# A scan and a bilinear feed-forward on one core: half of pair 1's B on GpSimd's load queue, third weights and middle rows behind its first mask

## The chip, the core and the metric

The kernel runs on one core of a Trainium2 chip. The metric is the device time of one execution in microseconds (us). The core has five engines with queues of their own: TensorE (PE, with its weight loads shown as PEld), VectorE (DVE), ScalarE (ACT), GpSimd (POOL) and SyncE (SP). Each works through its instructions in the order in which the program lists them and waits on semaphores for what other engines and transfers deliver. Transfers from memory (DMA) are issued by SP, ACT and GpSimd, and all three share the core's 16 DMA engines. In the profile a name with q behind it (SPq, ACTq) is the engine's sequencer.

## The reference

There are two parts, the second on the output of the first. With batch 4, 8 heads, 768 positions, head size 32 and state size 16:

```
log_a = log(clip(a, 1e-6, 1))
per chunk of 32 positions:
    cum  = cumsum(log_a of the chunk)
    L    = exp(cum_i - cum_j), lower triangle
    y    = ((C B^T) * L) x + (C state) * exp(cum)
    state = exp(sum log_a) * state + sum_j exp(cum_last - cum_j) B_j x_j
z   = y as 3072 tokens of 256 (head, dim)
out = ((z w_a) * (z w_b)) w_out        w_a, w_b: 256 x 1536, w_out: 1536 x 256
```

Inputs and the output are float32. The kernel computes products in float16 with float32 sums.

## The kernel before, in words

The 768 positions are cut in six blocks of 128 (`NBLK`); a block of two batches is a *pair*, so pairs 0 and 1 are block 0, pairs 2 and 3 are block 1, and so on up to pair 11. Decays come from a running product of `a` along a block (`scan`, line 250, on DVE) divided by its value in the middle (`over_mid`, line 253). For a pair, B and C are scaled by these factors (`scale_bc`, line 333, tiles `bm` and `cm`), turned on TensorE (`transposes`, line 374), multiplied to scores (`scores`, line 404) and masked (`mask`, lines 446 to 449). A mask is done by DVE straight from PSUM, or by GpSimd, and then ACT first copies the scores to `tmp`. The masked scores times x (`pv_u`, line 458) give `py`, and `evac0` (lines 563 and 565) copies it as float16 to `X2T`, on ACT or on DVE. From there the feed-forward takes units of 256 of the 1536 columns: `unit_mm` (line 598) makes `aps` with Wa and `bps` with Wb, `evac_a` (line 612) copies the one, `times` (line 622) multiplies both, and `out_mm` (line 637) multiplies with Wo.

The order of the work is written out by hand: the schedule is manual, and an engine does what is listed in the order of the listing. Four things in it matter here.

The loads come first. SP loads `a` and halves of pair 0's and pair 1's B (`bn`) and C (`cn`); ACT loads the other halves, five transfers, and then its activation table. GpSimd loads x of pair 0 in two halves (`xn`, 64 KB each), the first halves of Wa and Wb (384 KB each in float16), x of pair 1 in two halves, and the second half of Wa. Behind its first mask it loads the second half of Wb. In the calls `load1(engine, pair, which, half)`, which is 0 for B, 1 for C and 2 for x, and two further numbers limit a load to some rows.

Block 1 has layouts of its own: `load_q` loads its B and C (`bq`, `cq`) on SP. The first of these transfers is made to wait for the first half of Wa by a dependence on `w0`. `scale_q` (line 346, GpSimd) scales them into `planes`, `turn` (line 359, DVE) transposes them, and `scores(2)` uses them. `mid_rows` (line 288, GpSimd, tile `Ps`) makes the factors of block 1 and later, which `turned_rows` transposes. `clear` (line 294, GpSimd) sets the unused columns of the planes to zero.

Warmups (line 238) are matmuls of constants that nothing reads; they fill TensorE's queue at fixed places.

PSUM banks of the feed-forward are dealt out by the string `BANKS`: the n-th call of `bank` takes the n-th digit's bank, and a new user of a bank waits for the readers of the one before. The first calls are fps, tb, tc, py0, py1, and then aps of the first three units.

Of the kernel before, what the change touches and what calls it, by code (L numbers as in the profile page):

```python
# [19 lines left out]
SS = 64.0  # L20

BANKS = (
    "012313213212312312031203123021032103120312013201320130231021302130231203120312013023102310"
    "2312013201320132012301230123012301230123012301320132013201320132013201320132013201320"
)


# [1 line left out]
def kernel(  # L29
# [13 lines left out]
    nc = tc.nc  # L43
# [34 lines left out]
    Wa = [big.tile([128, 2, KC], f16, name=f"Wa{t}") for t in range(2)]  # L78
# [50 lines left out]
    def bank(name):  # L129
        return psf.tile([128, 512], f32, name=name, tag=f"ff{next(banks)}")  # L130
# [9 lines left out]
    def by_token(t_):  # L140
        return t_.rearrange("p h r n -> p (h r n)").rearrange("p (t h n) -> p t h n", t=2, h=H)

    def load1(eng, p, which, bt, i0=0, n=64, to=None):
        blk, bp = divmod(p, NBP)
        if p >= P2:
            return eng.dma_start(
                by_token(pair_in[p][which])[:, bt],
                (B, C, x)[which][2 * bp + bt, :, blk * Q : (blk + 1) * Q, :].rearrange("h q n -> q h n"),
            )
        src = (B, C, x)[which][2 * bp + bt, :, blk * Q + 2 * i0 : blk * Q + 2 * i0 + 2 * n, :]  # L150
        if to is None:
            to = pair_in[p][which]
        return eng.dma_start(
            to[64 * bt + i0 : 64 * bt + i0 + n].rearrange("i h r n -> i h (r n)"),
            src.rearrange("h (i r) n -> i h (r n)", r=2),
        )
# [3 lines left out]
    def load_q(eng, blk, parts=ALL_Q):  # L160
        if blk not in by_batch:
            by_batch[blk] = [inq.tile([128, H, 4, N], f32, name=n_, tag=n_) for n_ in ("bq", "cq")]
        return [
            eng.dma_start(
                by_batch[blk][w][32 * b : 32 * b + 32].rearrange("i h s n -> i h (s n)"),
                (B, C)[w][b, :, blk * Q : (blk + 1) * Q, :].rearrange("h (i s) n -> i h (s n)", s=4),
            )
            for w, b in parts
        ]
# [12 lines left out]
    def load_w(half, W):  # L182
        src = moe_w_a if W is Wa else moe_w_b
        c = slice(half * KC, (half + 1) * KC)
        return nc.gpsimd.dma_start(W[half], src.rearrange("(f p) e -> p f e", p=128)[:, :, c])
# [12 lines left out]
    load1(nc.scalar, 0, 1, 1)  # L198
    load1(nc.sync, 0, 1, 0, 0, 32)
    load1(nc.scalar, 0, 1, 0, 32, 32)  # L200
    for w in (1, 0):
        load1(nc.sync, 1, w, 0)
        load1(nc.scalar, 1, w, 1)
    nc.scalar.preload_act_table_set("natural_log_exp_and_others")
    nc.vector.memset(zero, 0.0)
    nc.gpsimd.memset(ident, 1.0)
# [21 lines left out]
    for p in range(2):  # L228
        for bt in range(2):
            load1(nc.gpsimd, p, 2, bt)  # L230
        if p == 0:
            w0 = load_w(0, Wa)
            load_w(0, Wb)
    load_w(1, Wa)

    def warmup(bank, *widths):
        for cols in widths:
# [10 lines left out]
    def scan(lo, hi):  # L248
        for k in range(lo, hi):
            nc.vector.tensor_tensor_scan(Pr[:, k], a_sb[:, k], zero, 1.0, ALU.mult, ALU.add)  # L250
# [4 lines left out]
    def sel_over_mid(lo, hi, eng):  # L255
        eng.tensor_tensor(
            out=selr[:, lo:hi].rearrange("p k t c -> p k (t c)"),
            in0=sel.rearrange("p t b h -> p (t b h)").unsqueeze(1).broadcast_to((BH, hi - lo, 2 * NBP * H)),
            in1=rmid[:, lo:hi].unsqueeze(2).broadcast_to((BH, hi - lo, 2 * NBP * H)),
            op=ALU.mult,  # L260
        )
# [24 lines left out]
    def mid_rows(lo, hi, eng):  # L286
        k = slice(lo + NBLK - NT, hi + NBLK - NT)
        eng.tensor_tensor(
            out=Ps[:, lo:hi], in0=Pr[:, k], in1=rmid[:, k].unsqueeze(2).broadcast_to((BH, hi - lo, Q)), op=ALU.mult
        )  # L290

    def clear(t_, eng):
        words = t_.rearrange("p c s -> p (c s)").bitcast(u32).rearrange("p (g w) -> p g w", g=3)
        eng.memset(words[:, 0:2, 32:96], 0)
# [29 lines left out]
    def scale_bc(p, which, eng, factor=None):  # L324
        blk, bp = divmod(p, NBP)
        name, f = (("bm", fB), ("cm", fC))[which]
        if p >= P2:
            f = (fBl, fCl)[which][:, blk - P2 // NBP].rearrange("p (b t h) -> p b t h", b=NBP, t=2)[:, bp]
        else:
            f = f[:, blk, :, bp]  # L330
        raw = by_token(pair_in[p][which]) if p >= P2 else pair_in[p][which].rearrange("p h r n -> p r h n")
        m_ = mid.tile([128, 2, H, N], f16, name=name, tag=name)
        eng.tensor_tensor(
            out=m_,
            in0=raw,
            in1=(f if factor is None else factor).unsqueeze(3).broadcast_to((128, 2, H, N)),
            op=ALU.mult,
        )
        st.setdefault(p, {})[name] = m_
# [94 lines left out]
    def product0(m2, e):  # L434

        return (
            st[0]["T1"][:, 2 * m2 : 2 * m2 + 2].rearrange("p m (e r) q -> p e m (r q)", e=2)[:, e],
            (SC0, SC1)[m2][:, :, e * 256 : e * 256 + 256],
            causal.rearrange("p r q -> p (r q)").unsqueeze(1).broadcast_to((128, 2, 2 * Q)),
        )  # L440

    def mask(out_in, by_pool=False):
        o_, i_, c_ = out_in
        if by_pool:
            tmp = mid.tile([128, *c_.shape[1:]], f32, name="tmp", tag="tmp")
            nc.scalar.copy(tmp, i_)  # L446
            nc.gpsimd.tensor_tensor(out=o_, in0=tmp, in1=c_, op=ALU.mult)  # L447
        else:
            nc.vector.tensor_tensor(out=o_, in0=i_, in1=c_, op=ALU.mult)  # L449
# [110 lines left out]
    def evac0(u, bt, eng, py):  # L560
        o_, i_ = X2T[:, 0, bt, u], py[bt][:, u * Q : (u + 1) * Q]
        if eng is nc.scalar:
            nc.scalar.activation(out=o_, in_=i_, func=AF.Copy, scale=YS / SS)
        else:
            nc.vector.tensor_scalar(o_, i_, YS / SS, None, ALU.mult)
# [218 lines left out]
    scale_bc(0, 1, nc.vector, v.rearrange("p (r b h) -> p r b h", r=2, b=NBP)[:, :, 0])  # L784
    over_mid(1, 2)
    sel_over_mid(1, 2, nc.vector)
    mid_rows(0, 1, nc.gpsimd)
    tb, tcp = bank("tb"), bank("tc")
    transposes(0, [tb, tcp], lambda: warmup(SC[3], 256))
    nc.scalar.copy(flat(fC, 0, 1), v)  # L790
# [3 lines left out]
    mask(product0(0, 0))  # L794
    mask(product0(0, 1))
    mask(product0(1, 1), by_pool=True)
    mask(product0(1, 0))
    clear(planes[0], nc.gpsimd)
    warmup(tcp, 512)
# [5 lines left out]
        evac0(0, bt, nc.scalar, py)  # L805
    warmup(tcp, 512, 128)
    scale_bc(1, 1, nc.vector)
    scan(4, 5)
    scale_bc(1, 0, nc.vector)
    clear(planes[1], nc.gpsimd)  # L810
    pv_u(0, 1, py, True)
    for bt in range(2):
        evac0(1, bt, (nc.scalar, nc.vector)[bt], py)
    load_w(1, Wb)
    for i_ in load_q(nc.sync, 1):
        tc.add_manual_dep(i_.ins, w0.ins.name, AFTER, reason="first weights ahead of block 1")
    for p in (2, 3):
# [249 lines left out]
```

## Time and profile before

| | |
|---|---|
| median of 3 runs | 122.99 us (122.61 to 123.38) |
| the profiled execution | 122.69 us |
| its span, first to last instruction | 120.8 us |
| PE busy | 115.9 us, 96% of the span |
| DVE, ACT, POOL busy | 90.2, 67.9, 58.8 us |
| granted TensorE clock | 1.000 |
| read from memory, written | 12.42 MB, 3.15 MB |

The span lies 1.9 us below the execution's time. Times in the timeline count from the start of the span. A row of the timeline gives start, duration, engine, line, operation, tiles, shapes and a count, and in brackets the idle time ahead of it with the engine or transfer that ended it. The table by stage gives, for each stretch, the busy time of every engine, the granted clock, the mean busy share of the 16 DMA engines and GB/s. Landing times are the time from the start of a DMA's issue until its data are there.

### The profile page before, as it was taken

The page shows a single profiled execution, that of the slowest core. Times are in us where ns is not written, and L with a number is a line of the kernel's source. Part 1 is how long each engine was busy: PE and PEld are TensorE (multiplying, and loading weights), DVE is VectorE, ACT ScalarE, POOL GpSimd, SP SyncE. Part 2 cuts the span into 40 slices and gives each one's busy share as a digit, 9 for nine tenths or more (in the row PEclk, how much of TensorE's full clock was granted, in tenths as well). Part 3 has the DMA queues.
Part 4 walks back from the last instruction along what each step waited for, and adds up shares of the span by engine and source line. Part 5 has one row for each costly group of instructions (what it writes and reads, how often), then busy time and mean ns, then how long its engine had stood idle before and what let it go on. Part 6 is the DMA issues. An engine that isn't in the chain of part 4 may idle for free.

```text
span 120.8 us, 3551 instructions
## 1 busy us (share of the span) xinstructions
PE 115.9 (96%) x1385; PEld 73.9 (61%) x1386; DVE 90.2 (75%) x166; ACT 67.9 (56%) x136; POOL 58.8 (49%) x92
## 2 busy tenths in 40 slices
PE   7989999999999999999999999999999999999990
PEld 2436789888644488544485464775465684645880
DVE  5998988999798994599966999686899426758000
ACT  0446756769776646567666646635735637475230
POOL 7994986999699969387803994200000000000000
PEclk9999999999999999999999999999999999999999
DMA  3999999894789994959992929012001111010132
GB/s 63 135 183 192 207 230 197 134 200 113 99 94 161 115 139 101 110 68 121 218 241 89 85 9 121 5 46 87 5 6 40 43 49 44 0 43 0 43 108 71
DMA packets 59297, 12.13 MB, mean 100 GB/s; under 512 B 54480, under 2 KB 59216, under 8 KB 59280
## 3 DMA queue, kind: packets, MB, share of 16 engines
q0 software_dynamic: 20320, 3.80, 38.9%
q1 hardware_dynamic: 36432, 7.74, 34.8%
q10 hardware_dynamic: 2528, 0.36, 1.8%
q8 instruction: 11, 0.18, 0.7%
q14 instruction: 6, 0.05, 0.1%
HBM read 12.42 MB, written 3.15 MB: 129 GB/s over the span
## 4 chain that ended last, share of the span: by engine, by line
PE 92%; DVE 4%; issue 0%; ACT 0%
PE ops L693 22%; PE aps L667 22%; PE bps L667 21%; PE ops L637 5%; PE aps L598 4%; PE SC L404 4%; PE bps L598 3%; DVE t L449 3%; PE SC L238 3%; PE SC L473 2%; PE SC L536 1%; PE tc L238 1%; PE py L458 1%; PE SC L485 1%; DVE bt L385 1%
## 5 line engine op out<-in xcount | busy, mean ns | idle before, releaser
L612 ACT COPY asb<-aps 128x512 f32<-128x512 f32 x72 | 42.0, 587 | 17.2 <-PE aps L667 13.4
L679 DVE TENSOR_TENSOR hkb<-bps,asb 128x512 f16<-128x512 f32 x60 | 40.2, 687 | 12.7 <-ACT asb L612 11.1
L667 PE MATMUL aps<-XB,Wa 128*128 128x512 f16 x120 | 35.7, 379 | 0.0
L667 PE MATMUL bps<-XB,Wb 128*128 128x512 f16 x120 | 35.7, 379 | 0.0
L693 PE MATMUL ops<-Wo,hkb 128*128 128x256 f16 (+1 forms) x252 | 28.1, 268 | 0.0
L693 PEld LDWEIGHTS <-hkb 128*128 128x128 f16 x252 | 23.0, 98 | 3.8
L667 PEld LDWEIGHTS <-Wb 128*128 128x128 f16 x120 | 12.4, 103 | 13.6
L667 PEld LDWEIGHTS <-Wa 128*128 128x128 f16 x120 | 12.1, 103 | 11.7 <-issue 0.5
L449 DVE TENSOR_TENSOR t<-SC,causal_q 128x512 f16<-128x512 f32 x27 | 17.3, 681 | 2.4 <-PE SC L404 2.4
L705 ACT ACTIVATE osb<-ops 128x256 f32<-128x256 f32 (+1 forms) x20 | 7.6, 379 | 18.4 <-PE ops L693 18.4
L447 POOL TENSOR_TENSOR t<-tmp,causal_q 128x512 f16<-128x512 f32 x5 | 5.8, 1161 | 10.0 <-ACT tmp L446 10.0
L177 POOL DMA_DIRECT2D xn<-in_x_dram x8 | 9.5, 1192 | 0.0
L346 POOL TENSOR_TENSOR planes<-cq,FC 128x256 f16<-128x256 f32 x10 | 7.6, 775 | 2.2 <-DMA cq<-in_C_dram 2.1
L622 DVE TENSOR_TENSOR hk<-bps,asb 128x512 f16<-128x512 f32 x11 | 7.2, 672 | 0.9 <-ACT asb L612 0.8
L346 POOL TENSOR_TENSOR planes<-bq,FB 128x256 f16<-128x256 f32 x10 | 7.7, 772 | 0.4 <-DMA bq<-in_B_dram 0.4
L449 DVE TENSOR_TENSOR t<-SC,causal 128x512 f16<-128x512 f32 x11 | 7.0, 675 | 0.4 <-PE SC L404 0.3
L598 PE MATMUL aps<-X2T,Wa 128*128 128x256 f16 x48 | 6.8, 274 | 0.0
L446 ACT COPY tmp<-SC 128x512 f32<-128x512 f32 x10 | 5.9, 589 | 1.5 <-PE SC L404 1.1
L598 PE MATMUL bps<-X2T,Wb 128*128 128x256 f16 x48 | 6.6, 273 | 0.0
L558 ACT ACTIVATE XB<-SC 128x512 f16<-128x512 f32 (+1 forms) x9 | 4.6, 547 | 3.5 <-PE SC L501 2.4
L447 POOL TENSOR_TENSOR t<-tmp,causal 128x512 f16<-128x512 f32 x5 | 5.8, 1161 | 0.0
L637 PE MATMUL ops<-Wo,hk 128*128 128x256 f16 x48 | 5.8, 273 | 0.0
(101 smaller groups left out, 109.2 us busy)
## 6 DMA issues: line engine op xcount, KB each, us to landing
out_dram<-osb SPq DMA_DIRECT2D x23, 128.0 KB, 1.8
cq<-in_C_dram SPq DMA_DIRECT2D x20, 64.0 KB, 3.9
bq<-in_B_dram SPq DMA_DIRECT2D x18, 64.0 KB, 3.8
bn<-in_B_dram SPq DMA_DIRECT2D x8, 128.0 KB, 4.1
xn<-in_x_dram POOLq DMA_DIRECT2D x8, 128.0 KB, 5.9
Wa<-in_moe_w_a_dram POOLq DMA_DIRECT2D x2, 384.0 KB, 7.3
Wb<-in_moe_w_b_dram POOLq DMA_DIRECT2D x2, 384.0 KB, 7.9
Wo<-in_moe_w_out_dram POOLq DMA_DIRECT2D x2, 384.0 KB, 6.5
```

The costliest lines, as they stand in the source:

```text
L177: eng.dma_start(by_token(pair_in[p][which]).rearrange("p t h n -> p (t h) n"), src.rearrange("t h q n -> q (t h) n"))
L346: eng.tensor_tensor(out=plane[:, c0 : c0 + 4 * step].rearrange("p (j c) s -> p j s c", c=step)[:, :, :, 0:N], in0=by_batch[blk][which][:, ...
L447: nc.gpsimd.tensor_tensor(out=o_, in0=tmp, in1=c_, op=ALU.mult)
L449: nc.vector.tensor_tensor(out=o_, in0=i_, in1=c_, op=ALU.mult)
L598: nc.tensor.matmul(ps[:, kk * 2 * Q : (kk + 1) * 2 * Q], W[k // 6][:, f, k % 6 // 3 * 384 : (k % 6 // 3 + 1) * 384].rearrange("p (c kk) -> ...
L612: (nc.vector.tensor_copy if on_dve else nc.scalar.copy)(asb, a_ps)
L622: eng.tensor_tensor(out=s["hk"][:, 2 * k2 : 2 * k2 + 2, :].rearrange("p k q -> p (k q)"), in0=b_ps, in1=asb, op=ALU.mult)
L637: nc.tensor.matmul(o_ps[:, 0:d_model], hk[:, k, bt * Q : (bt + 1) * Q], Wo[:, k, :], start=(k == 0), stop=(k == NK - 1), skip_group_check= ...
L667: nc.tensor.matmul(t_, W[k // 6][:, f, k % 6 // 3 * 384 : (k % 6 // 3 + 1) * 384].rearrange("p (c kk) -> p kk c", kk=3)[:, k % 3], XB[:, b ...
L679: return lambda: nc.vector.tensor_tensor(out=s["hk"][:, k], in0=ps[1], in1=asb, op=ALU.mult)
L693: nc.tensor.matmul(o_ps[:, 0:w], hk[:, k, c * Q : (c + 1) * Q], Wo[:, k, cs], start=(k == 0), stop=(k == NK - 1), skip_group_check=True,)
L705: nc.scalar.activation(out=o_sb[:, 0:w], in_=o_ps[:, 0:w], func=AF.Copy, scale=1.0 / (YS * YS))
```

## The change

Three things change, and the banks' string with them. Of pair 1's loads, the second half of B goes from ACT's queue to GpSimd's, where it stands behind pair 0's x and ahead of the first half of Wa; the half of C that ACT loads is issued as two transfers of 32 rows each; SP keeps its two. On GpSimd, the load of the second half of Wa moves from the end of the first loads to behind the first mask, and `mid_rows(0, 1)`, until now ahead of that mask, moves behind the load of the second half of Wb. On DVE, `scan(4, 5)`, until now between the scalings of pair 1's C and B, moves behind the last copy of pair 0 to `X2T`. In `BANKS`, the banks of the second and third aps are exchanged (seventh and eighth digit); the rest is the same pattern of reuse with banks named otherwise.

```
 BANKS = (
-    "012313213212312312031203123021032103120312013201320130231021302130231203120312013023102310"
-    "2312013201320132012301230123012301230123012301320132013201320132013201320132013201320"
+    "012313123121321321032103213012031203210321023102310230132012301230132103210321023013201320"
+    "1321023102310231021302130213021302130213021302310231023102310231023102310231023102310"
 )
...
     load1(nc.scalar, 0, 1, 0, 32, 32)
-    for w in (1, 0):
-        load1(nc.sync, 1, w, 0)
-        load1(nc.scalar, 1, w, 1)
+    load1(nc.sync, 1, 1, 0)
+    load1(nc.scalar, 1, 1, 1, 0, 32)
+    load1(nc.scalar, 1, 1, 1, 32, 32)
+    load1(nc.sync, 1, 0, 0)
...
             load1(nc.gpsimd, p, 2, bt)
         if p == 0:
+            load1(nc.gpsimd, 1, 0, 1)
             w0 = load_w(0, Wa)
             load_w(0, Wb)
-    load_w(1, Wa)
...
     sel_over_mid(1, 2, nc.vector)
-    mid_rows(0, 1, nc.gpsimd)
     tb, tcp = bank("tb"), bank("tc")
...
     mask(product0(1, 1), by_pool=True)
+    load_w(1, Wa)
     mask(product0(1, 0))
     clear(planes[0], nc.gpsimd)
...
     scale_bc(1, 1, nc.vector)
-    scan(4, 5)
     scale_bc(1, 0, nc.vector)
     clear(planes[1], nc.gpsimd)
     pv_u(0, 1, py, True)
     for bt in range(2):
         evac0(1, bt, (nc.scalar, nc.vector)[bt], py)
+    scan(4, 5)
     load_w(1, Wb)
+    mid_rows(0, 1, nc.gpsimd)
     for i_ in load_q(nc.sync, 1):
```

More of the change, by code (lines that the diff above doesn't have):

```diff
@@ L22 @@
 BANKS = (
-    "012313213212312312031203123021032103120312013201320130231021302130231203120312013023102310"
-    "2312013201320132012301230123012301230123012301320132013201320132013201320132013201320"
+    "012313123121321321032103213012031203210321023102310230132012301230132103210321023013201320"
+    "1321023102310231021302130213021302130213021302310231023102310231023102310231023102310"
 )
@@ L200 @@
     load1(nc.scalar, 0, 1, 0, 32, 32)
-    for w in (1, 0):
-        load1(nc.sync, 1, w, 0)
-        load1(nc.scalar, 1, w, 1)
+    load1(nc.sync, 1, 1, 0)
+    load1(nc.scalar, 1, 1, 1, 0, 32)
+    load1(nc.scalar, 1, 1, 1, 32, 32)
+    load1(nc.sync, 1, 0, 0)
     nc.scalar.preload_act_table_set("natural_log_exp_and_others")
@@ L231 @@
         if p == 0:
+            load1(nc.gpsimd, 1, 0, 1)
             w0 = load_w(0, Wa)
             load_w(0, Wb)
-    load_w(1, Wa)
     def warmup(bank, *widths):
@@ L786 @@
     sel_over_mid(1, 2, nc.vector)
-    mid_rows(0, 1, nc.gpsimd)
     tb, tcp = bank("tb"), bank("tc")
@@ L796 @@
     mask(product0(1, 1), by_pool=True)
+    load_w(1, Wa)
     mask(product0(1, 0))
@@ L807 @@
     scale_bc(1, 1, nc.vector)
-    scan(4, 5)
     scale_bc(1, 0, nc.vector)
@@ L813 @@
         evac0(1, bt, (nc.scalar, nc.vector)[bt], py)
+    scan(4, 5)
     load_w(1, Wb)
+    mid_rows(0, 1, nc.gpsimd)
     for i_ in load_q(nc.sync, 1):
```

## The prediction

> **What bounds the kernel now.** I read the page first: the shares by engine, then the chain that ended last.
>
> ```profile
> span 120.8 us, 3551 instructions
> PE 115.9 (96%) x1385; PEld 73.9 (61%) x1386; DVE 90.2 (75%) x166; ACT 67.9 (56%) x136; POOL 58.8 (49%) x92
> ...
> PE 92%; DVE 4%; issue 0%; ACT 0%
> ```
>
> TensorE is busy for 115.9 of 120.8 us, and 92% of the chain is PE. Whatever is done on other engines can win only what PE still waits. A table by stage says where that is:
>
> ```profile
> core 0: us, PE busy (x) PEld busy (x) DVE busy (x) ACT busy (x) POOL busy (x), PEclk, DMA share, GB/s
> ...
> 8.00:11.00 3.00, 2.87 (x48) 1.59 (x47) 2.71 (x7) 1.15 (x4) 2.38 (x6) 1.00 1.19 201
> 11.00:14.80 3.80, 3.66 (x102) 2.88 (x100) 3.64 (x9) 3.04 (x7) 2.65 (x5) 1.00 1.42 197
> 14.80:22.00 7.20, 7.17 (x81) 6.34 (x80) 6.18 (x14) 4.36 (x9) 5.59 (x12) 1.00 1.14 212
> 22.00:41.00 19.00, 18.93 (x295) 12.49 (x295) 17.76 (x31) 14.07 (x31) 17.66 (x25) 1.00 1.03 128
> 41.00:117.00 76.00, 76.00 (x797) 47.38 (x796) 53.77 (x89) 42.66 (x81) 23.41 (x31) 1.00 0.62 74
> ```
>
> Each row is a stretch, its length, then busy time per engine. PE's gaps sum to 0.13 + 0.14 + 0.03 + 0.07 us from 8 us on, and to nothing after 41. The edits all act between 3 and 12 us, so the gain that could exist is a few tenths of a microsecond. Third, the timeline of the stretch in question:
>
> ```profile
> 8.01 1.15 POOL L447 TENSOR_TENSOR t<-tmp,causal 128x512 f16<-128x512 f32 x1
> ...
> 9.37 0.41 DVE L250 TENSOR_TENSOR_SCAN Pr<-a_sb,zero 32x128 f32<-32x128 f32 x1
> ...
> 9.70 0.39 DVE L333 TENSOR_TENSOR bm<-bn,fB 128x256 f16<-128x256 f32 x1
> ...
> 10.02 0.27 DVE L565 TENSOR_SCALAR X2T<-py 128x128 f16<-128x128 f32 x1
> 10.14 0.11 PEld L374 LDWEIGHTS <-bm 128*128 128x128 f16 x2 [0.42 <-DVE bm L333]
> ```
>
> GpSimd's mask of pair 0 ends at 9.16; asked for PE alone, the timeline has 15 of the 16 products of L458 starting at 9.38, behind a first one at 9.21, so the mask holds them back. Pair 1's `bm` ends at 10.09 and PE's transposes of it start at 10.14. Fourth, the way of each load, asked by tile (issue plus time to landing): pair 1's second B half is issued on ACT at 3.60 and lands at 9.6, Wa's first half 4.06 and 9.8, Wb's first 4.76 and 11.8, pair 1's x 12.6, Wa's second 6.83 and 15.7, Wb's second 9.40 and 18.1, block 1's last C 11.23 and 19.1, its last B 14.81 and 20.3.
>
> **The change, part by part.**
>
> *ACT's queue.* It loses one 64 KB B load (0.65 us of issue) and gets its 64 KB C load in two of 32 KB. Its 32 KB load of now lies among three C loads that take 2.00 together, 0.67 each, so a half costs as much as a whole: -0.65 + 0.65 = 0. The table load still starts near 4.28, and ACT's first use, the copy at 6.06, stays. The C halves, issued by 4.25, must land by 8.99 (`cm` of pair 1); the whole one landed at 6.9 after 3.9 us, and 4.25 + 3.9 = 8.2 still does. [...]
>
> *GpSimd's queue up to the mask.* Now: x 2.51 and 3.38, Wa, Wb, x twice, Wa at 6.83 (0.76), then middle rows at 7.65 (0.39), then the mask at 8.01. It gains a B load (0.69, from the x loads beside it) behind the first two, and loses the 0.76 and the 0.39. Issues then end at 6.83 + 0.69 = 7.5; the mask waits for its copy `tmp` (7.17 + 0.59 = 7.76) and starts near 7.84 where it was 8.01: **0.17 earlier**. The other half of its product is DVE's mask, and PE's first product, which needs only that, is at 9.21 as before; so the 15 move from 9.38 to about 9.24, **-0.14** on PE.
>
> *The B load.* On ACT's queue its last packets drag on beside the weights: between 7 and 9.5 us that queue (q10) still moves 144 packets.
>
> ```profile
> q0 software_dynamic: 322, 0.47, 108.4%
> q10 hardware_dynamic: 144, 0.02, 7.6%
> ```
>
> On GpSimd's queue it comes behind x and ahead of Wa. A trace of it does not exist; bounds: as x's second load, 3.9 us from 4.07 is 8.0; as pair 1's x, 6.5 to 6.7 behind two weights, is 10.8. I take 8.2, as only x lies ahead of it. Then `bm` need not wait, and with the scan (0.41) moved behind it starts at 9.37 and ends at 9.76, not 10.09. The X2T copy at 10.02 comes to 9.77 and the scan to about 10.0, off the path: its reader, `rmid`, is at 11.62, and DVE idled 0.29 before 10.58. PE's transposes are then bound by the products and the two warmups ahead of them, and keep the -0.14: 10.00. If `bm` had stayed, the -0.14 would end here.
>
> *Wa and Wb behind it.* 64 KB more on their queue, and the drag of 7.6% of 2.5 us = 0.19 gone. When this queue has the engines alone it moves 795 packets in 0.7 us (11.0 to 11.7), so 512 take 0.45: net **+0.26** later; the bounds are 0 (the bytes moved before Wa lands are the same in both orders, as the B half landed before it) and +0.55. Wa lands at 10.1; its first product, 10.38 now, would be at 10.24. No wait at the value taken, at the upper bound 0.1. Wb lands at 12.0; its first load into PE is at 12.05 now, 11.9 then: 0.1 of waiting, which is covered because the next products (L458 at 13.86) wait for masks that end at 13.81. At +0.55 the cover is gone and 0.2 to 0.3 is paid.
>
> *Third weights behind the mask.* Issue from 8.99 to 9.75, where Wb's clears then follow (0.34) and the fourth weights start at 10.1, not 9.40; middle rows (0.39) end by 11.3, the last clear (0.23) by 11.5, and the next operation behind them, `hr`, starts at 11.87 now after 1.49 of idle: covered, without which it were 0.76. Both weights are still issued before pair 1's x has left the queue (landing 12.6), so the queue never runs dry. Wa's second half is due at 17.85, 2.1 us after its landing; Wb's second at 19.16, 1.0 after. SP issues block 1 when Wa's first half has landed (9.85), 0.26 later; its C lands 7.5 to 7.9 us after issue, with the weights on their way all that time. I take 0, bounds -0.3 to +0.4 for these landings.
>
> *Banks.* The new list swaps two entries, aps of units 1 and 2 of pair 0, and renames the rest. Unit 1 then writes where `py1` was, read last by the X2T copy (10.04); it starts about 10.7: 0.
>
> **Sum.** -0.14 reaches pair 1's scores, masks and the unit at 14.85, as each follows the one before on PE or DVE. But at 19.32 GpSimd waits for block 1's C from memory, and what follows is `turn` at 21.34 and PE's scores at 21.98:
>
> ```profile
> 19.32 1.37 POOL L346 TENSOR_TENSOR planes<-cq,FC 128x256 f16<-128x256 f32 x2 [1.38 <-DMA cq<-in_C_dram]
> ...
> 21.34 0.58 DVE L359 STREAM_TRANSPOSE turned<-planes 128x384 f32<-128x384 f32 x1
> ...
> 21.98 0.21 PEld L404 LDWEIGHTS <-turned 32*64 32x64 f16 x12 [0.21 <-DVE turned L359]
> ```
>
> PE's aps before it leaves no free time to speak of, so both chains meet here. If the C lands when it did, PE comes 0.14 early and waits 0.14. I keep a third: **-0.05**. The profiled execution took 122.69 (span 120.8 and 1.9 around it), so 122.64; the median of the runs shown is 122.99, 0.30 more, and a median is what is measured: 122.9.
>
> **Rivals.**
>
> *The gain is kept* (10%). If block 1's C lands 0.2 to 0.3 earlier, since it is queued nearer to the fourth weights, the whole -0.14 passes, with 0.1 from the waits at 22 to 41: 122.7. Against it: the bytes ahead of it are the same.
>
> *The fourth weights are overtaken* (12%), slower. They are issued at 10.1 to 10.9, SP's C loads from 9.9 or 10.1 on. If all of block 1's eight loads go first, the weights land last, at about 20.3, while PE needs them at 19.16 - 0.14: a stall of 1.2 to 1.3 us, less what the gate at 21.98 then gives back (at most 0.1): 124.1. It decides from the point where the landing is over 1.0 us later than 18.1. Against it: in the stretch from 10 to 13 us GpSimd's queue moved 1361 packets and SP's none, though four C loads and two B loads had been issued. [...]
>
> *The B half lands late* (6%): the change's purpose fails. At 10.8 `bm` starts 1.1 later than 9.70, and X2T's copy, the scan and `bt` queue behind it on DVE: PE's transposes and Wa's first products lose 1.1, 124.0. For it: pair 1's x loads on this queue; against: weights lay before those.
>
> *A real gain over 1%* (3%): PE's waits after 8 us sum to 0.4; it would need something the trace does not show: 121.6.
>
> **How the numbers follow.** No change, within 0.3 of 122.9, has 69%. About 1% is what a measurement of this kernel tells from no change. Faster by over that: 4%. Slower: the two slow rivals in full strength, cut to 11% as partial stalls (0.3 to 0.8) stay within. Same: 85%. The range is 122.1 (the kept gain, and the lowest run shown, 122.61, moved by 0.4) to 123.9 (the late rivals but for their last two tenths).
>
> **What would show it.** Right: GpSimd's mask starting near 7.84, `bm` near 9.37, the scan near 10.0, transposes near 10.0, scores of block 1 still close to 21.98 with PE waiting there for `turned`. Wrong: a wait of PE before L598 at 10.2 or 12, or at 19 for Wb; `bm` behind a DMA; block 1's C landing more than 0.3 from 19.1.

## The result, and the profile after

Over 17 runs the kernel after the change takes **123.65 us** in the median (122.88 to 127.33); the kernel before takes 122.94 (122.58 to 123.38). The ratio is 1.0055, with a 95% interval of 1.0031 to 1.0079: some 0.7 us **slower**, where 122.9 and "no change" had been forecast. Runs that lie more than 1.5% above a kernel's fastest are left out of all ratios here but not out of the medians; the execution that was profiled with the result (127.33 us) is one of those, so the comparison below uses an ordinary execution of the same kernel, 123.47 us, from experiment `e0_after`.

Its page: one row for the span, the shares by engine, the chain that ended last.

```profile
span 121.7 us, 3552 instructions
PE 116.4 (96%) x1385; PEld 74.2 (61%) x1386; DVE 90.3 (74%) x166; ACT 67.9 (56%) x136; POOL 59.5 (49%) x93
...
PE 78%; DMA 10%; POOL 4%; SPq 4%; issue 1%; DVE 0%; ACT 0%; POOLq 0%
```

The span grew by 0.8 us (121.67 less 120.85) and PE's work by 0.5. What matters is the last line: the chain was 92% PE, and now 18% of it are transfers, GpSimd and SP's queue. A chain that leaves PE and runs through SP's loads says that PE waited for them somewhere. The table by stage of the same execution, with the columns of before, says where:

```profile
8.00:11.00 3.00, 2.88 (x49) 1.54 (x47) 2.87 (x8) 1.00 (x5) 2.73 (x5) 1.00 1.14 200
11.00:14.80 3.80, 3.66 (x104) 2.94 (x101) 3.66 (x8) 3.08 (x7) 3.10 (x8) 1.00 1.36 173
14.80:22.00 7.20, 7.18 (x77) 6.47 (x78) 5.79 (x13) 4.51 (x10) 5.18 (x11) 1.00 1.16 216
22.00:41.00 19.00, 18.43 (x294) 12.23 (x293) 17.56 (x31) 13.56 (x31) 18.18 (x27) 1.00 1.19 137
```

From 8 to 22 us, where every edit acts, PE is as busy as before. It loses 0.57 of the 19 us behind 22, where before it lost 0.07. The last column of the second row is down from 197 to 173 GB/s: less is moved between 11 and 14.8. The timeline around 22, all engines but the queues:

```profile
19.90 1.38 POOL L347 TENSOR_TENSOR planes<-cq,FC 128x256 f16<-128x256 f32 x2 [1.69 <-DMA cq<-in_C_dram]
21.40 0.77 POOL L347 TENSOR_TENSOR planes<-bq,FB 128x256 f16<-128x256 f32 x1
22.20 0.58 DVE L360 STREAM_TRANSPOSE turned<-planes 128x384 f32<-128x384 f32 x1 [0.68 <-POOL planes L347]
22.84 0.58 PE L405 MATMUL SC<-turned 32*64 32x128 f16 x25 [0.53 <-DVE turned L360]
```

Read it from below (lines are one higher than before): PE's `scores(2)`, which were ready to go at 22.3, wait 0.53 for `turned`, and DVE waits for the `planes` made from B. These start behind the `planes` made from C, for which GpSimd had to wait until the last C of block 1 had landed. In the profile before the two rows start at 19.32 (shown with the prediction) and here:

```profile
20.54 0.77 POOL L346 TENSOR_TENSOR planes<-bq,FB 128x256 f16<-128x256 f32 x1
```

So `planes` from C start 0.58 later, at 19.90, as the last C landed at 19.74 and not at 19.16. `planes` from B then follow 1.50 behind them and not 1.22, as the last B landed at 21.19 and not at 20.33: 0.28 more. Together that is the 0.86 by which `scores(2)` start later, at 22.84 and not 21.98, and as much as the span grew. The larger part is the C, the smaller the B.

PE itself also came 0.33 late to `scores(2)`, which the wait hides. Of this, 0.26 is there at its first unit (10.64, not 10.38), behind two warmups at 6.12 that ran 0.93 instead of 0.60: the trace's record of the granted clock begins, at full clock, at 6.77 in this execution and at 5.08 in the one before, and a warmup of 512 columns took 0.58 to 0.63 ahead of it and 0.38 to 0.39 behind it (last section).

The slowest execution (span 125.6) shows the same place, and more of it:

```profile
15.28 0.76 POOL L188 DMA_DIRECT2D Wo<-in_moe_w_out_dram  x1
...
23.77 0.76 POOL L347 TENSOR_TENSOR planes<-bq,FB 128x256 f16<-128x256 f32 x1 [2.21 <-issue]
...
25.19 0.41 PE L405 MATMUL SC<-turned 32*64 32x128 f16 x14 [3.13 <-DVE turned L360]
```

Here SP issued the last B at 15.68, after GpSimd had issued the 384 KB of Wo at 15.28; it landed at 23.56, and PE waited 3.1 us. The last C had landed at 20.03. ("issue" in brackets only says that the view found no releaser; the landing of `bq` by its tile does.) In the ordinary execution the order was 15.04 for B and 15.37 for Wo.

### The profile page after: what moved, and what is told of

Its sections match the earlier page's. It is cut to its first block, busy times and chain, and to the rows that moved or that the text cites. A ratio compares the mean times of both kernels' runs of the same rounds, so it can differ in the third digit from the quotient of the medians.

```text
span 125.6 us, 3553 instructions
## 1 busy us (share of the span) xinstructions
PE 117.9 (94%) x1386; PEld 74.7 (59%) x1386; DVE 90.3 (72%) x166; ACT 67.9 (54%) x136; POOL 59.4 (47%) x93
## 4 chain that ended last, share of the span: by engine, by line
PE 77%; DMA 9%; SPq 4%; POOL 4%; issue 2%; DVE 0%; ACT 0%; POOLq 0%
PE ops L694 22%; PE aps L668 21%; PE bps L668 21%; PE ops L638 5%; DMA bq<-in_B_dram 5%; DMA Wa<-in_moe_w_a_dram 4%; SPq L164 4%; PE SC L405 3%; PE SC L474 2%; PE bps L599 1%; POOL xn L153 1%; PE SC L537 1%; PE aps L599 1%; POOL causal L226 1%; POOL planes L347 1%
## 5 line engine op out<-in xcount | busy, mean ns | idle before, releaser
L360 DVE STREAM_TRANSPOSE turned<-planes 128x384 f32<-128x384 f32 x10 | 5.5, 561 | 3.3 <-POOL planes L347 3.3
L405 PE MATMUL SC<-turned 32*128 32x128 f16 (+1 forms) x192 | 4.5, 217 | 3.1 <-DVE turned L360 3.1
L599 PE MATMUL bps<-X2T,Wb 128*128 128x256 f16 x48 | 7.2, 288 | 0.1
L405 PEld LDWEIGHTS <-turned 32*128 32x128 f16 (+1 forms) x192 | 2.8, 97 | 6.5 <-DVE turned L360 3.8
```

What stands on the lines that cost most here:

```text
L405: nc.tensor.matmul(o_, b_, c_, start=True, stop=True, skip_group_check=True, tile_position=at)
L599: nc.tensor.matmul(ps[:, kk * 2 * Q : (kk + 1) * 2 * Q], W[k // 6][:, f, k % 6 // 3 * 384 : (k % 6 // 3 + 1) * 384].rearrange("p (c kk) -> ...
```

## The experiments

Edits are against the kernel after the change unless the lead says "before". All are timed beside the kernel before. Listings are shortened; `...` stands for lines left out. A load's *landing* is issue plus time to landing from the tile's view. The questions came in this order: which part costs, through which load, and why.

**Which part.** The changed kernel again; then the kernel before with the moves of loads alone (pair 1's B half to GpSimd, C in two); then before with GpSimd's order alone (third weights and middle rows behind the mask, loads as they were).

> The changed kernel once more, for a second profile of it and as the mark for the three kernels beside it. In its first profile TensorE waits 3.3 us ahead of block 1's scores for the last B load of block 1, which SP issued at 15.68, just behind GpSimd's issue of Wo at 15.28, and which landed at 23.56. If that profile is the rule, the time is near 127; by its other runs it is near 123.5. Then the last B should be issued ahead of Wo, land near 21 to 21.4, and the wait ahead of the scores be 0.5 to 1.0 us.

1.0054 (1.0028 to 1.0081), median 123.78, with a tail at 124.48, 125.44, 126.59 and 127.72: the loss repeats, and with it a tail of single long runs.

```
 e1_loads_only, against before          e2_order_only, against before
-   for w in (1, 0):                    -   load_w(1, Wa)        # with the first loads
-       load1(nc.sync, 1, w, 0)         ...
-       load1(nc.scalar, 1, w, 1)       -   mid_rows(0, 1, nc.gpsimd)
+   load1(nc.sync, 1, 1, 0)             ...
+   load1(nc.scalar, 1, 1, 1, 0, 32)        mask(product0(1, 1), by_pool=True)
+   load1(nc.scalar, 1, 1, 1, 32, 32)   +   load_w(1, Wa)
+   load1(nc.sync, 1, 0, 0)             ...
...                                         load_w(1, Wb)
+   load1(nc.gpsimd, 1, 0, 1)           +   mid_rows(0, 1, nc.gpsimd)
    w0 = load_w(0, Wa)
```

> The kernel before with the moves of pair 1's loads alone (half of B to GpSimd's queue, half of C in two pieces). Theory 1, late start: the B half delays Wa's landing by 0.4 (9.83 to 10.24 in the changed kernel), SP's eight loads of block 1 start on that landing, so all of them come 0.4 later, the last one close to or behind Wo: this kernel shows the loss of 0.5 to 0.9 us. Theory 2, weights too late: the loss comes from issuing the third and fourth weights at 9.0 and 10.1, among SP's loads, not at 6.8 and 9.4: this kernel stays within 0.2 us of the kernel before.

> The kernel before with GpSimd's new order alone: third weights behind its first mask, middle rows behind the fourth weights. Theory 1: SP's loads start at 9.85 as before, so the time stays within 0.2 us of the kernel before. Theory 2: the last C of block 1 lands 0.5 or more later than 19.1 and the loss of 0.5 to 0.9 us is here.

Loads alone 1.0021 (1.0003 to 1.0040), order alone 1.0000 (0.998 to 1.0019). The order costs nothing by itself, the loads about 0.3 us; together, by the means, they cost more than the sum, though the interval of the loads alone overlaps with those of the changed kernel. The loads alone have no tail: their highest run is 123.76. In the profile of the loads alone Wa's first half landed at 11.21 and SP's block 1 started at 11.22, yet the last B was there at 20.77. The reverse test takes the moves of loads out of the changed kernel and leaves the order, the scan's place and the banks, twice:

```
-    load1(nc.sync, 1, 1, 0)
-    load1(nc.scalar, 1, 1, 1, 0, 32)
-    load1(nc.scalar, 1, 1, 1, 32, 32)
-    load1(nc.sync, 1, 0, 0)
+    for w in (1, 0):                    # pair 1's loads as before
+        load1(nc.sync, 1, w, 0)
+        load1(nc.scalar, 1, w, 1)
...
-            load1(nc.gpsimd, 1, 0, 1)
```

> The changed kernel with the loads of pair 1 as they were (B half whole on ACT behind its whole C half): what stays is GpSimd's new order, the scan's new place and the banks. Theory 1: the loss is gone, ratio 0.998 to 1.002, no run above 124. If the loss comes from the scan or from the banks, the only parts not yet tried by themselves, it stays at 1.003 to 1.007.

> The changed kernel with the loads of pair 1 as they were, a second time: 0.997 to 1.001, no run above 124 but at most one; faster than the kernel before only if the scan's and the weights' new places are worth something by themselves.

0.9990 (0.9974 to 1.0006) and 0.9991 (0.9974 to 1.0009), no run above 123.6: without the load moves there is no loss. The profile of the first shows what these were to remove, and that PE waits for it: `bm` late by a transfer (the columns are who waited, for whom, us in all, times, longest).

```profile
PE SC L373 <- DVE bm L332: 0.9, 1, 0.9
```

A second profile of the kernel before, and one more of the changed one, both unedited, show whether that wait is there as well and how much it varies:

> The changed kernel, the mark for the one with C whole: 1.003 to 1.008 as twice before, with some runs above 124. Its profile is one more sample: Wa's first half at 10.2 to 11.3 if the B half's place delays it.

> The kernel before as one of the four: ratio 0.998 to 1.002. Its profile is one more sample without the moves: Wa's first half at 9.8 to 10.4 and the B half on ACT's queue landing at 9.6 to 10.6, with a wait of TensorE for bm where it lands after 9.7.

The kernel before again: 0.9982 (0.9963 to 1.0001), median 122.92, one run of twelve above 124 (125.1). After again: 1.0041 (1.0013 to 1.0069), with 124.59, 126.58, 126.99 and 127.33 in its tail. In the profile of before, B's half landed at 10.27 instead of 9.63, and PE paid:

```profile
10.29 0.43 DVE L333 TENSOR_TENSOR bm<-bn,fB 128x256 f16<-128x256 f32 x1 [0.54 <-DMA bn<-in_B_dram]
...
10.77 0.28 PE L374 MATMUL SC<-ident,bm 128*128 128x128 f16 x2 [0.56 <-DVE bm L333]
```

**Through which load: SP's block 1.** SP's eight loads wait for the first half of Wa (`w0`). Let them wait for the B half on GpSimd's queue instead, which is early, or for the first half of Wb, which is late:

```
-            load1(nc.gpsimd, 1, 0, 1)          # e4
+            b11 = load1(nc.gpsimd, 1, 0, 1)
...
-        tc.add_manual_dep(i_.ins, w0.ins.name, ...)
+        tc.add_manual_dep(i_.ins, b11.ins.name, ...)   # e4; in e6 w1 = load_w(0, Wb)
```

> The changed kernel, but SP's loads of block 1 wait for the landing of the B half on GpSimd's queue (about 8.0), not for Wa's first half (about 10.3); each instruction keeps its place. Theory 1, late start: the loads come 2 us sooner, the last B is issued well ahead of Wo, block 1 lands sooner, and the time falls to 123.0 or below with no run above 124. Theory 3, mixing: block 1's loads slow the transfer when they are issued among the third and fourth weights; here all three stand together, so the weights land later than 16.0 and 18.7, TensorE waits for them after 18, and the time stays at 123.6 or rises.

> The changed kernel, but SP's loads of block 1 wait for the first half of Wb (about 12.2), 2 us later than in the changed kernel. Theory 1: the last B is always issued behind Wo, lands after it (23.4 or later), and the time is 126 to 128 in nearly every run, as in the slowest runs of the changed kernel. Theory 3: block 1's loads no longer mix with the weights, and what the late start costs is made good in part: 123.3 to 124.5.

Early: 1.0020 (0.9992 to 1.0049). In its profile the first load goes out at 8.27, the last B lands at 20.11, and `scores(2)` start at 22.09 without a wait; but the forecast of no run above 124 failed. Late: **1.0211** (1.0161 to 1.0260); the first load at 12.89, the last B issued at 16.48, behind Wo at 15.89, and landed at 23.50.

```profile
PE SC L405 <- DVE turned L360: 2.4, 1, 2.4
```

A start 1.9 us later than Wa's landing (11.02) makes the tail of the changed kernel the rule: the dependence is a path to the long waits. It does so through the last B alone. The last C landed at 19.40 here, earlier than in the changed kernel (19.58 to 20.03 in its three profiles), though it was issued at 14.38, later than in any of them. The early start is not a cure: 4 of its 12 runs lie above 124.2, for a reason that stays open.

**Wo.** If it is Wo that overtakes the last B, then a later Wo must remove the tail. It is issued in turn behind `batch_factors` (0.95 us later) or behind `mid_rows(1, NT)` as well:

```
-    load_wo(0)
     ...
     batch_factors(0, 1, *range(nb), eng=nc.gpsimd)
+    load_wo(0)                             # e7
     mid_rows(1, NT, nc.gpsimd)
+    load_wo(0)                             # e3, instead
```

> The changed kernel with the first half of Wo issued behind the four copies of factors, so 0.95 us later (near 16.1). It tells what the runs above 124 are. If they are those in which Wo is issued ahead of the last B of block 1, they vanish (highest run under 124.2) and the median falls to 123.1 to 123.4, Wo still landing before its first use at 24. If not, runs above 124 stay at about one in four.

> The changed kernel with the first half of Wo issued behind the second middle rows (near 17.3), not ahead of the factors (15.3). Theory 1, in its part about the order of issue: the last B of block 1 can no longer fall behind Wo, so the runs above 124 vanish and the time comes to 122.9 to 123.2, unless Wo, first used at 23.8, lands too late. Theory 2: Wo is not what delays block 1, and the time stays near 123.5.

Behind the copies: 1.0032 (1.0005 to 1.0060), no run above 125, where the changed kernel has 7 of 41; but 124.36 and 124.92 are above the 124.2 that was forecast as the limit. The last C landed at 19.21 and the last B at 20.03, with no wait at `scores(2)`. Behind the middle rows as well: 1.0105 (1.0063 to 1.0146); the last B at 20.41 and again no wait there, but PE lost 1.0 us for Wa (landed at 11.31) and, through block 2's loads (the last B landed at 35.38, before at 31.99), as much at a further `turned`, at 37 us:

```profile
PE SC L405 <- DVE turned L360: 1.0, 1, 1.0
PE aps L599 <- DMA Wa<-in_moe_w_a_dram: 1.0, 1, 1.0
```

So the long waits come where Wo is issued ahead of the last B: by 0.4, 0.3 and 0.6 us in the three profiles with one, where B lands at 23.2 to 23.6. (In `e12_c_whole_again` Wo is ahead by 0.01 only, and B lands at 21.57.) In both profiles with a later Wo, B landed near 20 and nothing waited there. That it takes the tail away is likely, but 12 and 6 runs do not show it, and pushed back far enough Wo only moves the waits. What is left in the first of the two is a wait for Wa, 0.6 at PE's first unit.

**The fourth weights, ahead of their clears**, to keep GpSimd's queue full between 10 and 11 us, as the drop from 197 to 173 GB/s between 11 and 14.8 us might come from there:

```
     load_w(1, Wa)
+    load_w(1, Wb)          # no longer behind the scales and clears
```

> The changed kernel with the fourth weights issued directly behind the third, so near 9.8 and not 10.1 to 10.4, about 0.5 ahead of SP's first load as in the kernel before. Theory 3: block 1's loads stand behind all weights again, the last C lands within 0.3 of 19.1, and the time comes to 123.0 to 123.2. Theory 1: SP starts as late as in the changed kernel, and the time stays near 123.6 with runs above 124.

1.0036 (1.0010 to 1.0063), with 125.17, 127.06 and 127.85 in its tail. It does not undo the loss. In its profile Wa landed at 10.81, nothing waited at `scores(2)`, and the rate from 11 to 14.8 us is 180 GB/s; the intervals of this kernel and the changed one overlap, so it neither helps nor harms by what these runs can tell.

**B on other queues.** The half behind SP's own half, instead of on GpSimd; and both halves on GpSimd, ahead of Wa, which doubles the 64 KB put before it:

```
-            load1(nc.gpsimd, 1, 0, 1)          # e9
+    load1(nc.sync, 1, 0, 1)                    # e9, behind SP's half
...
             load1(nc.gpsimd, 1, 0, 1)
+            load1(nc.gpsimd, 1, 0, 0)          # e11; SP's half goes
```

> The changed kernel with the B half issued by SP behind its own half, not by GpSimd: the same bytes at about the same time (issue near 4.0), no longer in Wa's queue. Theory 1 (place in the queue): Wa's issue is back at 4.06, it lands at 9.8 to 10.3, SP starts block 1 near 10, and the ratio falls to 0.998 to 1.002. Rival (the bytes, not the place): Wa lands at 10.2 to 11.2 as in the changed kernel and the ratio stays above 1.003. If the B half lands later than 9.4 here, the wait shows ahead of bm.

> The dose doubled: the changed kernel with SP's half of pair 1's B on GpSimd's queue as well, behind the other half and ahead of Wa. Theory 1: Wa is issued 0.7 later once more and lands at 10.7 to 11.5, TensorE waits for it, SP starts block 1 later still, and the ratio is 1.008 to 1.020. Rival (the place does not matter): the ratio stays at 1.003 to 1.007.

On SP: 1.0265 (1.0224 to 1.0306). Issued at 4.88, the half landed at **12.43**, and `bm` took PE with it:

```profile
12.53 0.43 DVE L334 TENSOR_TENSOR bm<-bn,fB 128x256 f16<-128x256 f32 x1 [3.07 <-DMA bn<-in_B_dram]
...
13.01 0.29 PE L375 MATMUL SC<-ident,bm 128*128 128x128 f16 x2 [2.73 <-DVE bm L334]
```

Wa landed at 9.89 there, as with no B ahead of it. Both on GpSimd: 1.0022 (1.0000 to 1.0043), Wa at 11.27, and one run above 124.1 (126.57).

```profile
PE aps L599 <- DMA Wa<-in_moe_w_a_dram: 0.7, 1, 0.7
```

That speaks against the simplest theory, a price per byte put ahead of Wa on its queue: with double the bytes 1.008 to 1.020 was forecast, and the ratio is not larger but rather smaller. PE came late to `scores(2)` by itself (23.02), so the last B at 21.44 cost nothing more.

**C in one piece**, twice, and then with the early start of SP's loads; and that with Wo ahead of the `times` of GpSimd:

```
-    load1(nc.scalar, 1, 1, 1, 0, 32)           # e8, e12, e15, e16
-    load1(nc.scalar, 1, 1, 1, 32, 32)
+    load1(nc.scalar, 1, 1, 1)
...
+    load_wo(0)                                 # e16 only, with b11 as in e4 and e15
     times(0, 1, bps[1], asb[1], by_pool=True)
-    load_wo(0)
```

> The changed kernel with ACT's half of pair 1's C in one piece. So far Wa's first half landed at 10.2 to 11.3 in eight profiles with the B half ahead of it and at 9.8 and 10.5 in two without. Theory 1 in its present form: the B half's place ahead of Wa delays Wa; the C pieces have no part in it, Wa lands at 10.2 or later and the ratio stays between 1.003 and 1.007. [...]

> The changed kernel with ACT's half of pair 1's C whole, a second time, beside the changed kernel on the same chip. If the split makes the loss: 1.000 to 1.002 here, 1.004 to 1.008 there, and no run above 124 here. If the B half's place makes it: both 1.003 to 1.006.

> C whole, the B half on GpSimd's queue, and SP's loads of block 1 waiting for that B half (8.0) and not for Wa. If SP's wait for Wa carries the loss to block 1, this is the fastest of the four with the move, 0.997 to 1.001; if starting early only mixes block 1's loads with the weights, 1.001 to 1.004 with runs above 124.

> C whole, the B half on GpSimd's queue, SP's loads of block 1 started by its landing, and the first half of Wo issued ahead of GpSimd's product of unit 1 (near 13.9, not 15.4). If the late Wo made the runs above 124, they vanish and the median is 122.5 to 122.9, ratio 0.996 to 0.999. If not, about a third of the runs stay above 124.

C whole: 1.0014 (0.9989 to 1.0039) and 1.0028 (0.9999 to 1.0057), against 1.0055, 1.0054 and 1.0041 with two pieces. All means lie lower, but the intervals overlap, and both profiles still show PE waiting 0.6 and 0.5 at `scores(2)`; that the two pieces cost something is possible and not shown. Wa landed at 10.59 and 10.94, so its landing does not come back with the whole C. (The 10.2 to 11.3 named with the first of these runs for the B half ahead of Wa leaves out the 9.81 of the early start.) With the early start: 1.0013 (0.9977 to 1.0050), but in two groups, seven runs from 122.52 to 123.0 and five from 124.04 to 125.52. An earlier Wo was to tell whether Wo makes the upper group. This kernel is slower in every run, 1.0138 (1.0105 to 1.0171): PE waited for Wa (landed at 11.34) and for pair 1's x (14.73 and 15.90).

```profile
PEld L458 <- DMA xn<-in_x_dram: 1.1, 2, 0.9
```

Wo is not shown to be the reason: it was issued at 14.78, when Wa and the first half of x had already landed late. With SP's loads started early, pair 1's x landed at 13.09, 14.25 and 15.90 in the three profiles, elsewhere at 12.62 to 14.06, so that x may make the upper groups; the profiles of the other two kernels are of runs of 122.73 and 122.54 us and cannot tell. What separates the groups stays open. No version came out below the kernel before by more than its interval.

## Why the prediction was wrong, point by point

**Right: the B load.** It was given a landing of 8.2 (7.82 to 8.48 in the thirteen profiles with just this half on GpSimd) and `bm` a start near 9.37. The timeline of the result's own execution has `bm` at 9.31, the X2T copy at 9.85 (9.77 forecast) and PE's transposes at 10.05 (10.00); the scan came at its forecast, near 10. ACT, the clears and `hr`, each taken at 0, show nothing on PE's path, and Wb's wait is 0.3 on PE's weight loads and covered. (The halves of C took 0.47 and 0.57 to issue, not as much as the whole with its 0.61, so ACT's loads were out by 4.06, not 4.25. Nothing hangs on it.)

```profile
7.91 1.15 POOL L448 TENSOR_TENSOR t<-tmp,causal 128x512 f16<-128x512 f32 x1 [0.36 <-ACT tmp L447]
...
8.88 0.45 ACT L564 ACTIVATE X2T<-py 128x128 f16<-128x128 f32 x2 [1.12 <-PE py L459]
...
9.21 0.47 PE L459 MATMUL py<-t,xn 64*32 64x128 f16 x16
9.31 0.42 DVE L334 TENSOR_TENSOR bm<-bn,fB 128x256 f16<-128x256 f32 x1
...
10.05 0.27 PE L375 MATMUL SC<-ident,bm 128*128 128x128 f16 x2
```

**Wrong: GpSimd's mask, and the -0.14 taken from it.** It started at 7.91, 0.1 and not 0.17 earlier, and of the -0.14 nothing came: the first product still starts at 9.21, the other 15 within the same 0.47 us, as before. The mask of GpSimd was not what held them. It had ended at 9.06 here and at 9.16 before, and the second product starts at 9.37 and 9.38. What ends just ahead of that in both profiles are ACT's two copies of `py` to `X2T`, from 8.88 to 9.33, and by the semaphores in the trace the second product waited for them. No run tests this. The 0.09 that PE gained at its transposes (10.14 to 10.05) came from `bm`.

**Wrong: Wa's landing was taken from one execution.** The rise of 0.26, with bounds of 0 and 0.55, was too small by half but within its bounds: Wa's first half lands at 10.24 in the mean of five profiles with the loads as before and at 10.76 in the thirteen with the B half ahead of it. But the base was 9.83, and the five are 9.83, 10.45, 10.32, 10.41 and 10.17: the execution shown had the earliest of them, and the earliest B (9.63, where the others have 9.84 to 10.57). So the cover was mis-sized twice. "No wait at the value taken" fails: in seven of the thirteen PE waits 0.1 to 1.0 for it. And what the move can win is larger than the one trace showed, since two of the five wait 0.6 and 0.9 for `bm` on PE and a third 0.2. The two cancel: PE's first unit starts at 10.80 in the mean of the five and at 10.88 of the thirteen. The move exchanged a wait for B for a wait for Wa.

**The step that failed: "I take 0, bounds -0.3 to +0.4 for these landings".** These are the landings of block 1's loads. The last C landed at 19.74 in `e0_after` and at 20.03 in the result's own execution, against 19.16: 0.58 and 0.87 later, beyond the upper bound. Over several executions it is 19.12 in the mean of the five profiles without the moves (18.82 to 19.30) and 19.84 in the mean of four ordinary ones with both parts of the change (19.63 to 20.01): 0.7 and not 0. "Block 1's C landing more than 0.3 from 19.1" was named as a sign of being wrong, and it came. The last B behind it was never priced: 20.33 before, 21.19 and 23.56 here. Nor was Wo, which GpSimd issues only 0.3 us after that B (14.81 and 15.11 in the kernel before). That 0.3 was the slack ahead of the long waits, and no row of the plan had it. The prediction did name the gate, PE's `scores(2)` at 21.98, as the place where both chains meet, so what was missing was the size of these landings.

For the 0 the prediction gave only that the C lands 7.5 to 7.9 us after its issue. The runs do not bear this out: the last C took 8.07 us in `e0_after`, 8.39 in the result's own execution, 5.54 in `e13_after_again` and 5.02 in `e6_late_start`. Nor did SP's issue just move by 0.26. Where SP waits for Wa, its first load of block 1 goes out at 10.84 in the mean of nine profiles with the move and at 10.25 of five without, and the last B is issued at 15.0 to 16.0 instead of 14.7 to 14.9. But this start does not explain the late C by itself: in the first two profiles of the changed kernel it is 10.25 and 10.31, within the 9.85 to 10.46 of the five without the moves, and with a start at 12.89 the C landed at 19.40. SP's own issues, four C and four B in three executions: the kernel before, `e0_after` and `e13_after_again`.

```profile
9.85 1.83 SPq L164 DMA_DIRECT2D cq<-in_C_dram  x4
11.72 3.54 SPq L164 DMA_DIRECT2D bq<-in_B_dram  x4
```

```profile
10.31 1.86 SPq L164 DMA_DIRECT2D cq<-in_C_dram  x4
12.21 3.28 SPq L164 DMA_DIRECT2D bq<-in_B_dram  x4
```

```profile
10.85 3.65 SPq L164 DMA_DIRECT2D cq<-in_C_dram  x4
14.54 1.93 SPq L164 DMA_DIRECT2D bq<-in_B_dram  x4
```

The last of the three took 126.99 us. Its last B goes out at 16.02 and Wo at 15.70; it lands at 23.24 and PE waits 2.3, though its last C landed at 19.58.

That 123.65 still lies within the range given, 122.1 to 123.9, is luck: none of the rivals describes it. (Its lower end is off in the sum too: 122.61 less 0.4 is 122.2.) The fourth weights landed at 18.65 in `e0_after` (18.14 before) without a wait of PE, and the B half was early.

**What is shown, and what is argued.** Shown: without the load moves there is no loss (0.999 twice), and the order by itself has none (1.0000). A late start of SP's loads puts the last B behind Wo and costs 2% (1.0211). What delays `scores(2)` delays the end: from their start to the end of the span it is 98.3 to 99.1 us in sixteen of the twenty profiles, and longer only where a wait of 1 us or a lower clock follows. `scores(2)` start at 22.42 in the mean of the five profiles without the moves and at 22.85 in the four ordinary ones with both parts of the change (one of them with the fourth weights sooner, two with C whole): 0.4 of the 0.7 us. PE is ready for them at 22.42 and 22.45; what differs is its wait for `turned`, 0.01 and 0.39. By their rows that wait is the late C in the main, with 0.1 to 0.3 from the last B in three of the four.

Only argued: why the C lands later, and why it takes both parts. The rate from 11 to 14.8 us behaves alike: 197 and 194 GB/s in the kernel before, 196 with the loads alone, 185 to 190 in three with the order alone, but 170 to 180 in all nine with both and one B half ahead of Wa, where SP does not start early. With both B halves there it is 195. No run shows that this drop is the cause. Also argued is that the rest of the 0.7 us is the tail, such as 124.48 and 124.59.

## What to carry to other kernels

A load moved forward can move another back: here a wait for B was traded for a wait for Wa, and the gain has to be looked for on the load that is now behind. Follow not just who reads that load but all loads that are still to land when a gate opens, and which load of another queue is issued next to the last of them; here the slack against a long wait was the distance between these two issues, 0.3 us in the kernel before (14.81 and 15.11). One profile gives one landing time; where the spread over executions (0.6 us here) is larger than the slack, take several before a stall is costed at nothing.

## What the runs showed of the hardware

In the profile before, the 20 loads that ACT, GpSimd and SP issued from 3.60 to 20.10 us landed in the order of their issue over all three queues, but for one: SP's first C of block 1, issued at 9.85, landed at 17.37, ahead of GpSimd's fourth weights, issued at 9.40 and landed at 18.14. From 10 to 13 us of that profile all 1361 packets were of GpSimd's queue, and SP's loads moved none. The same 64 KB of B took 7.55 us from SP in `e9_b_on_sp` (4.88 to 12.43), behind the two 384 KB loads of GpSimd, and 3.8 to 4.4 from GpSimd ahead of them (3.93 in the result's execution, 4.05 to 7.98).

The waits of 2.3 to 3.1 us at `scores(2)` cost PE more than their length. In the result's execution (span 125.6), the granted clock (third column from the right) is still 1.00 for 0.9 us behind the 3.1 us wait, and then 0.50:

```profile
22.00:25.20 3.20, 0.07 (x3) 0.01 (x2) 0.64 (x2) 0.59 (x1) 1.41 (x3) 1.00 0.77 140
25.20:26.10 0.90, 0.90 (x35) 0.80 (x36) 0.90 (x2) 0.17 (x1) 0.82 (x3) 1.00 1.22 102
26.20:29.50 3.30, 3.30 (x18) 2.32 (x17) 3.24 (x7) 1.82 (x5) 3.15 (x4) 0.50 1.02 170
29.60:45.00 15.40, 15.40 (x242) 9.63 (x241) 12.85 (x22) 10.87 (x25) 14.31 (x22) 1.00 1.23 117
```

By the trace's clock record the 0.50 lasts from 26.15 to 29.56, 3.41 us, which at 0.50 are an estimated 1.7 us of work: a further 1.7 on top of the wait. The span bears it out: from `scores(2)` to its end it is 100.4 us in the three profiles with such a drop behind them, and 98.3 to 99.1 in sixteen without. In `e13_after_again`, after 2.3 us of waiting, the granted clock is 0.50 for 3.41 us as well.

The first microseconds differ between executions as well. In all twenty profiles the record of the granted clock begins at full clock between 3.65 and 6.84 us, at no fixed time. A warmup of 512 columns took 0.58 to 0.63 us ahead of it and 0.38 to 0.39 behind it. (The clock column of the table by stage shows 1.00 there all the same.) In two executions of the changed kernel, the result's and `e0_after`, the record begins at 5.67 and 6.77 and PE's first unit starts at 10.28 and 10.64: a few tenths without any edit.
